# Three edits to a fused attention and expert kernel: every high half of the exponentials on ScalarE, one instruction for both biases of a query unit, and router logits by 8 products of 16 columns

## The chip, the cores and the metric

The kernel runs on one core of a Trainium2 chip. The metric is the device time of one execution in microseconds, as the median of several runs; the profile is one further execution with its own time. PE is the matrix engine (PEld its loading of weights), DVE the vector engine, ACT the scalar engine, POOL the general engine, SP the engine whose queue issues the DMAs here.

## The reference, cut to what matters

Three stages follow each other: linear attention over 4 batches of 8 heads with 576 tokens, a gated MLP, and a mixture of 8 experts with one expert per token.

```python
proj = x @ w_phi                                   # 64 -> 128, for q and for k
proj = proj - max(abs(proj), axis=-1)
phi = concatenate([exp(proj), exp(-proj)])
num = phi(q) @ (phi(k).T @ v);  den = phi(q) . sum(phi(k)) + 1e-6
x = num / den
xn = x / rms(x) * rms_g
x = (silu(xn @ w_gate) * (xn @ w_val)) @ w_out
logits = x @ w_gate2 + modality_bias[modality_id]  # 512 -> 8
out = gate * (relu(x @ w1[e]) @ w2[e])             # e = argmax(logits)
```

## The kernel before, in words

Values that need more than 16 bits are carried as a pair of float16 tiles, a high half (the value cast to float16) and a low half (the value minus its high half), and a product of two pairs is three matmuls: high by high, high by low, low by high. The function `split` (L146 to L152) makes such a pair: the cast on DVE (`hi="v"`, L149) or on ACT (`hi="a"`, L151), then the subtraction on DVE (L152).

**Attention.** Per batch there are 9 key units (`k_unit`) and 9 query units (`q_unit`), each with 4 blocks of 128 features in one bank of the matrix engine's output memory. A key unit takes the largest absolute value on DVE, subtracts it, and ACT takes the two exponentials of half a unit at a time (L301, L302). A query unit takes the maximum (`absmax`, L215), DVE makes two bias columns from it, `b1` = -3 times and `b2` = -1 times the maximum (L351, L352), and ACT takes 4 times 2 exponentials with these biases (L358, L359). Each half unit is then split. For batches 0 and 1 all casts of these splits are on ACT; for batches 2 and 3, by the table `EXP_SPLIT`, the first half unit's cast is on DVE and the second's on ACT. In batch 1 the keys are not split, in batch 0 and 1 all queries are. A DMA transpose (L365, `eT<-eq`) turns the split query unit around, and `oo` multiplies it with the key sums.

**MLP.** Tokens go in 9 groups of 256. Per group and block of 128 of the 1536 hidden features, `m1_mm` does 24 matmuls of 256 columns into `gv` (L520), and `m1_act` makes the hidden block: tanh on ACT (`th`, L527), two products on DVE (`th` L528, `hu` L530), and a split (`hT`). `gv` has two buffers, and the second product `hu` is the last reader of each. `m1_out_mm` multiplies with `w_out` (L542), `m1_evict` and `m1_store` write the result as a pair and transpose it (`x2T`), and `m1_logits` makes the router's logits of 128 tokens by 12 matmuls of 8 columns (L568) and one DVE instruction (L570) that scales and adds the bias table `lgb`. There are 18 such tiles of 128 tokens.

**Weights.** The MLP's weights are unpacked beside batch 0 and 1 (`wst`, `wu`, `wgv`, `wo`). The experts' weights come in 128 pieces, each loaded (`w2a`), cast on ACT (L635), reduced to its low half on DVE (L636), and stored (`w2b`), from batch 1 to the end of the MLP. All DMAs but the experts' gather and scatter are issued by SP in order.

**Experts.** A routing block on DVE sorts the tokens; then 20 or more slots of 128 tokens go through `mm1` (L978) and `mm2` (L994).

**Order.** `_weave` mixes the lists of steps of attention, MLP and weights by fixed shares, and the framework then schedules the whole program by a simulated timeline: the order of each engine's instructions is that schedule's, not the code's. Each engine takes its instructions in that order.

Of the kernel before, what the change touches and what calls it, by code (L numbers as in the profile page):

```python
# [8 lines left out]
F32 = mybir.dt.float32  # L9
# [3 lines left out]
ALU = mybir.AluOpType  # L13
# [9 lines left out]
NE = 8  # L23
# [9 lines left out]


CONV_LO = "v"
EXP_SPLIT = ('av', 'av', 'vv av', 'vv av')
PREP_LO = ('v', 'v', 'v', 'v')
NKV = 8
NXG = 2
# [23 lines left out]
def body(ctx, tc, k0, kt0, q0, qt0, kk, kkt, qq, qqt, vv, vvt, w_phi, w_gv, w_out, rms_g, mid, w_g2, mbias,  # L63
         w1, w2, consts, out):
    nc = tc.nc
    V, A, G, SP, PE = nc.vector, nc.scalar, nc.gpsimd, nc.sync, nc.tensor
# [4 lines left out]
    ps_ko = ctx.enter_context(tc.tile_pool(name="ps_ko", bufs=2, space=PSUM))  # L71
# [7 lines left out]
    def C(name, shape, dt=F32):  # L79
        return cp.tile(shape, dt, name=name)  # L80
# [5 lines left out]
    g_bc = C("g_bc", [128, DM])  # L86
    epsb = C("epsb", [128, 1])
    mhalf = C("mhalf", [128, 1])
    wg32 = C("wg32", [128, 4, NE])
    wg16 = C("wg16", [128, 4, 2, NE], F16)  # L90
    mid_i = C("mid_i", [128, NT, 2], I32)
# [2 lines left out]
    lgb = C("lgb", [128, NT, NE])  # L94
    lg = C("lg", [128, NT, NE])
# [5 lines left out]
    SP.dma_start(out=wp32, in_=w_phi)  # L101
    V.memset(epsb, math.log(0.25e-6))
    V.memset(mhalf, -0.5)

    def small_loads():
        SP.dma_start(out=cst, in_=consts)
        SP.dma_start(out=g_bc, in_=rms_g.rearrange("(o d) -> o d", o=1).to_broadcast([128, DM]))
# [103 lines left out]
    def small(tag, n, bufs=4):  # L211
        return apx.tile([128, n], F32, tag=tag, bufs=bufs, name=tag)

    def absmax(p, m):
        V.tensor_reduce(out=m, in_=p, axis=AX.X, op=ALU.max, apply_absolute_value=True)  # L215

    def attention(b, banks, eng, pp_lo):

        f32 = b == 0
        k32 = b == 1  # L220
        sc = 1.0 if f32 else 0.0625
        t, m, kvs, x = {}, {}, {}, {}
# [3 lines left out]
        def bank():  # L226
            pool, tag = banks[cnt[0] % len(banks)]
            cnt[0] += 1
            return pool.tile([128, 4, 128], F32, tag=tag, name="pj")

        def esplit(hi, lo, src):
            h, l = eng[lo_cnt[0] % len(eng)]
            lo_cnt[0] += 1
            split(hi, lo, src, hi=h, lo=l)
# [89 lines left out]
        def q_unit(p, rp):  # L324

            pp = bank()
            a = t["q", p]
            if p == 4:
                for i in range(4):
                    if f32:  # L330
                        PE.matmul(pp[:, i, :], lhsT=a[:, 128 * i:128 * i + 128], rhs=wp32[0:64, 0, :], start=True, stop=True)
                    else:
                        PE.matmul(pp[:, i, :], lhsT=a[:, i, :], rhs=wpA, start=True, stop=False)
                        PE.matmul(pp[:, i, :], lhsT=a[:, i, :], rhs=wpB, start=False, stop=True)
                mm, ppv, sh = m["t"], pp, lambda y: y
            else:
                for r in range(2):
                    if f32:
                        c = 128 * (2 * rp + r)
                        PE.matmul(pp[:, 2 * r:2 * r + 2, :], lhsT=a[:, c:c + 128], rhs=wp32, start=True, stop=True)  # L340
                    else:
                        for i in range(2):
                            l = a[:, 4 * i + 2 * rp + r, :]
                            PE.matmul(pp[:, 2 * r + i, :], lhsT=l, rhs=wpA, start=True, stop=False)
                            PE.matmul(pp[:, 2 * r + i, :], lhsT=l, rhs=wpB, start=False, stop=True)
                mm = m["m"][:, 2 * rp:2 * rp + 2, 2 * p:2 * p + 2]
                ppv = pp.rearrange("p (r h) f -> p r h f", h=2)
                sh = lambda y: y.rearrange("p (r h) -> p r h", h=2)
            absmax(ppv, mm)
            b1, b2 = small("b1", 4), small("b2", 4)  # L350
            V.tensor_scalar(out=sh(b1), in0=mm, scalar1=-3.0 * sc, scalar2=None, op0=ALU.mult)  # L351
            V.tensor_scalar(out=sh(b2), in0=mm, scalar1=-sc, scalar2=None, op0=ALU.mult)  # L352
            eq = ap.tile([128, 2, 4, 2, FEAT], F16, tag="E4", bufs=4, name="eq")
            for half in range(2):
                e = ap.tile([128, 2, 2, FEAT], F32, tag="e32", bufs=2, name="e32")
                for r in range(2):
                    j = 2 * half + r
                    A.activation(out=e[:, r, 0, :], in_=pp[:, j, :], func=AF.Exp, scale=sc, bias=b1[:, j:j + 1])  # L358
                    A.activation(out=e[:, r, 1, :], in_=pp[:, j, :], func=AF.Exp, scale=-sc, bias=b2[:, j:j + 1])  # L359
                sl = slice(2 * half, 2 * half + 2)  # L360
                esplit(eq[:, 0, sl], eq[:, 1, sl], e)
            tag, bufs = ("E4", 4) if cnt[1] % 3 else ("eX", 1)
            cnt[1] += 1
            o = ap.tile([128, 16, 128], F16, tag=tag, bufs=bufs, name="eT")
            SP.dma_start_transpose(out=o, in_=eq.rearrange("p a r s f -> p (a r s f)"))  # L365
            t["eT", p, rp] = o
            if p == 4:
                m["t2"] = apx.tile([64, 4], F32, tag="mt2", bufs=2, name="mt2")
                SP.dma_start(out=m["t2"], in_=m["t"][64:128])
# [88 lines left out]
        for n, h in enumerate(order + [None]):  # L458
            pre = []
            if h is not None and h < 8:  # L460
                p = h // 2
# [15 lines left out]
        def q_steps(rp):  # L477
            st = []
            for p in range(5):
                fs = []  # L480
                if p < 4:
                    fs.append(L(q_unit, p, rp))
                    if rp == 0:
                        if p + 1 < 4:
                            fs.append(L(prep, "q", p + 1))
                        if p + 2 < 4:
                            fs.append(L(load, "q", p + 2))
                    elif p == 0:
                        fs.append(L(load, "q", 4))
                    elif p == 1:  # L490
                        fs.append(L(prep, "q", 4))
                if p < 4:
                    st.append(seq(*fs))
                elif rp == 1:
                    st += [L(q_unit, 4, 0)]
                if p >= 2:
                    st.append(L(oo, p - 2, rp))
            if rp == 1:
                st.append(tail_m)
            st.append(L(oo, 3, rp))  # L500
            st += [seq(L(norm, 2 * rp)), seq(L(norm, 2 * rp + 1), L(ntr, 2 * rp)), L(ntr, 2 * rp + 1)]
            return st
# [58 lines left out]
    def m1_logits(g, i):  # L561
        t = state.pop(("x2T", g, i))
        tt = 2 * g + i
        p = ps_ko.tile([128, NE], F32, tag="ko", name="lgp")
        n = 0
        for kc in range(4):
            for xl, wl in ((0, 0), (0, 1), (1, 0)):
                mm = PE.matmul(p, lhsT=t[:, 4 * xl + kc, :], rhs=wg16[:, kc, wl, :], start=(n == 0), stop=(n == 11))  # L568
                n += 1
        V.scalar_tensor_tensor(out=lg[:, tt, :], in0=p, scalar=1.0 / 1024.0, in1=lgb[:, tt, :],  # L570
                               op0=ALU.mult, op1=ALU.add)
        return mm.ins

    def out_steps(g):
# [12 lines left out]
    def group_steps(g, prev):  # L587

        st = []
        for c in range(12):  # L590
            st.append(lambda c=c: m1_mm(g, c, 0))

            def s(c=c):
                m1_mm(g, c, 1)
                m1_act(g, c)
                if prev is not None:
                    if c == 2:
                        m1_store(prev, 1)
                    if c == 4:
                        m1_logits(prev, 0)  # L600
                    if c == 6:
                        m1_logits(prev, 1)
            st.append(s)
            if c == 1 and prev is not None:
                st += out_steps(prev)
        return st
# [444 lines left out]
    bk = list(wide)  # L1051
    att = [attention(b, bk if b == 0 else narrow, EXP_SPLIT[b].split(), PREP_LO[b]) for b in range(4)]
    done = [0]
# [21 lines left out]
    for b in range(4):  # L1075
# [8 lines left out]
        n = KSPLIT * len(ks) // 100  # L1084
# [9 lines left out]
        n = len(wst) // 2  # L1094
# [14 lines left out]
    n = len(w2s) * M7 // (M7 + 12)  # L1109
# [6 lines left out]
    for s in out_steps(8):  # L1116
        s()
    m1_store(8, 1)
    last = [m1_logits(8, 0), m1_logits(8, 1)]
    moe_ctx.close()  # L1120
    rpools.append(ctx.enter_context(tc.tile_pool(name="rp2", bufs=1, reuse_waits="tile")))
# [90 lines left out]
```

## Time and profile before

| | us |
|---|---|
| median of 3 runs | 919.63 |
| lowest, highest | 914.98, 919.82 |
| profiled execution | 923.65 |
| span of the profile in it | 921.9 |
| busy PE, DVE, ACT in the span | 814.6, 592.9, 431.7 |
| mean granted TensorE clock | 0.935 |

The profiled execution took 1.75 us more than its span, and 4.0 us more than the median. By stage: until about 95 us the attention of batch 0 with little else on PE, until 256 us the MLP of the first groups beside batch 1 and the MLP's own weights, from 256 us to 546 us the MLP beside the keys and queries of batches 2 and 3 and the experts' weights, until 702 us the rest of the MLP, routing and weights, and from then on the experts.

### The profile page before, as it was taken

Reading aid. Unit: us, or ns where it says so; the run is one execution under the profiler, and the core shown is the slowest. Engines: PE = TensorE matmul, PEld = TensorE weight load, DVE = VectorE, ACT = ScalarE, POOL = GpSimd, SP = SyncE. Lnnn points to the kernel's source line nnn. Section 1 sums busy time; section 2 is a strip of 40 time slices with the busy share of each in tenths; the row PEclk is TensorE's granted clock in tenths of the full one; section 3 lists DMA queues with packets and bytes.
Section 4 is the critical chain, followed back from the end, with each engine's and each line's share of the span. In section 5 each row is a group of like instructions: output and inputs, shape, how many; then the busy total and the mean of one; then the engine's idle time right before and its main releaser. Section 6 shows DMA issues by size and latency. Waiting matters only on the chain. (4 is left out here: it accounts for less than half of the span.)

```text
span 921.9 us, 18413 instructions
## 1 busy us (share of the span) xinstructions
PE 814.6 (88%) x6840; PEld 559.0 (61%) x6840; DVE 592.9 (64%) x1448; ACT 431.7 (47%) x1125; POOL 86.8 (9%) x104
## 2 busy tenths in 40 slices
PE   5745789988899998989998979998899998999995
PEld 5534588767577776666786667675674443444442
DVE  6989898996778877869987866456835411122121
ACT  4787555585656665757767744234321111111110
POOL 0001030000130000210000102000010221211010
PEclk8656699999989999999999989999999999999998
DMA  8589978599989799899879986897896499698732
GB/s 268 146 193 217 206 154 207 164 196 234 212 209 260 238 242 241 199 232 242 215 221 232 226 223 190 311 356 247 235 379 136 114 233 217 130 303 240 173 71 52
DMA packets 266589, 197.38 MB, mean 214 GB/s; under 512 B 212863, under 2 KB 214271, under 8 KB 262912
## 3 DMA queue, kind: packets, MB, share of 16 engines
q1 hardware_dynamic: 263296, 186.21, 79.3%
q0 software_dynamic: 3200, 9.97, 3.4%
q8 instruction: 55, 0.90, 0.4%
q14 instruction: 38, 0.31, 0.1%
HBM read 164.92 MB, written 43.52 MB: 226 GB/s over the span
## 5 line engine op out<-in xcount | busy, mean ns | idle before, releaser
L520 PEld LDWEIGHTS <-wgv 128*128 128x128 f16 x2592 | 257.4, 101 | 71.8 <-issue 23.5
L520 PE MATMUL gv<-xT,wgv 128*128 128x256 f16 x2304 | 281.2, 281 | 19.2 <-DVE hu L530 11.8
L542 PE MATMUL po<-wo,hT 128*128 128x512 f16 x648 | 152.1, 380 | 0.3
L635 ACT ACTIVATE w2b<-w2a 128x512 f16<-128x512 f32 x128 | 80.9, 632 | 114.3 <-DMA w2a<-in_w_dram 107.5
L636 DVE SCALAR_TENSOR_TENSOR w2b<-w2a,w2b 128x512 f16<-128x512 f32 x128 | 88.6, 692 | 70.2 <-ACT w2b L635 69.9
L994 PE MATMUL m2y<-L,hsT 128*128 128x512 f16 x480 | 108.4, 383 | 3.9 <-DMA hsT<-hs 3.9
L981 ACT ACTIVATE hs<-m2h 128x512 f16<-128x512 f32 x40 | 23.9, 597 | 180.8 <-PE m2h L978 180.8
L978 PE MATMUL m2h<-L,xT 128*128 128x512 f16 x480 | 107.0, 379 | 0.8 <-DMA L<-ws 0.5
L542 PEld LDWEIGHTS <-hT 128*128 128x128 f16 x648 | 61.2, 98 | 62.7 <-DVE hT L152 1.2
L994 PEld LDWEIGHTS <-hsT 128*128 128x128 f16 x480 | 47.2, 99 | 62.1 <-DMA hsT<-hs 5.1
L978 PEld LDWEIGHTS <-xT 128*128 128x128 f16 x480 | 46.6, 98 | 57.4 <-issue 1.4
L982 DVE SCALAR_TENSOR_TENSOR hs<-m2h,hs 128x512 f16<-128x512 f32 x40 | 27.6, 691 | 79.7 <-ACT hs L981 75.9
L423 POOL TENSOR_TENSOR x<-x,g_bc 128x512 f32<-128x512 f32 x16 | 22.0, 1373 | 483.4 <-ACT xg L422 482.7
L387 PE MATMUL oo<-kv,eT 128*128 128x65 f16 x768 | 33.0, 204 | 35.4 <-DMA eT<-eq 30.1
L151 ACT CAST hT<-hu 128x256 f16<-128x256 f32 x108 | 43.7, 406 | 32.4 <-DVE hu L530 31.1
L528 DVE SCALAR_TENSOR_TENSOR th<-th,gv 128x256 f32<-128x256 f32 x108 | 44.7, 414 | 20.7 <-ACT th L527 20.3
L358 ACT ACTIVATE e<-pj,b 128x128 f32<-128x128 f32 x144 | 55.3, 384 | 4.8 <-DVE eq L152 2.2
L359 ACT ACTIVATE e<-pj,b 128x128 f32<-128x128 f32 x144 | 56.2, 390 | 0.0
L387 PEld LDWEIGHTS <-eT 128*128 128x128 f16 x768 | 30.0, 104 | 42.6 <-DMA eT<-eq 36.5
L527 ACT ACTIVATE th<-gv 128x256 f32<-128x256 f32 x108 | 41.5, 384 | 28.5 <-PE gv L520 28.3
L318 PE MATMUL kv<-vs,ek 128*128 128x65 f16 (+1 forms) x720 | 43.2, 206 | 13.0 <-DVE ek L152 9.9
L152 DVE TENSOR_TENSOR eq<-e,eq 128x512 f16<-128x512 f32 x72 | 52.0, 727 | 3.6 <-ACT eq L151 3.3
(226 smaller groups left out, 1066.2 us busy)
## 6 DMA issues: line engine op xcount, KB each, us to landing
L<-ws SPq DMA_DIRECT2D x88, 1024.0 KB
w2a<-in_w_dram SPq DMA_DIRECT2D x128, 256.0 KB
ws<-w2b SPq DMA_DIRECT2D x128, 256.0 KB
wst<-in_w_gv_dram SPq DMA_DIRECT2D x24, 512.0 KB
wst<-in_w_out_dram SPq DMA_DIRECT2D x12, 512.0 KB
xs<-x SPq DMA_DIRECT2D x18, 256.0 KB
v<-in_vv_dram SPq DMA_DIRECT2D x16, 260.0 KB
k<-in_kk_dram SPq DMA_DIRECT2D x12, 256.0 KB
```

Of the source, the lines that this page charges most:

```text
L151: A.copy(dst_hi, src)
L152: (V if lo == "v" else G).tensor_tensor(out=dst_lo, in0=src, in1=dst_hi, op=ALU.subtract)
L358: A.activation(out=e[:, r, 0, :], in_=pp[:, j, :], func=AF.Exp, scale=sc, bias=b1[:, j:j + 1])
L359: A.activation(out=e[:, r, 1, :], in_=pp[:, j, :], func=AF.Exp, scale=-sc, bias=b2[:, j:j + 1])
L387: PE.matmul(acc[:, j, :], lhsT=et[:, hl * 8 + j * 2 + s, :], rhs=kvs[2 * p + j % 2][:, vl, s, :], start=(n == 0), stop=(n == 5))
L520: PE.matmul(p[:, which, :], lhsT=w[:, kc, wl, f], rhs=x[:, 4 * xl + kc, :], start=(n == 0), stop=(n == 11))
L528: V.scalar_tensor_tensor(out=t, in0=t, scalar=1.0, in1=p[:, 0, :], op0=ALU.add, op1=ALU.mult)
L542: PE.matmul(p, lhsT=hT[g, c][:, hl, tk], rhs=wo[:, c, wl, :], start=(c == 0 and hl == 0 and wl == 0), stop=(c == 11 and hl == 1))
L635: A.activation(out=o[:, :, 0, :], in_=t, func=AF.Copy, scale=WS)
L636: V.scalar_tensor_tensor(out=o[:, :, 1, :], in0=t, scalar=WS, in1=o[:, :, 0, :], op0=ALU.mult, op1=ALU.subtract)
L978: PE.matmul(p, lhsT=x[:, 4 * xl + kc, :], rhs=w[:, kc, half, wl, :], start=(n == 0), stop=(n == 11))
L994: PE.matmul(p, lhsT=t[:, 4 * hl + i, :], rhs=w[:, fc, wl, :], start=(fc == 0 and hl == 0 and wl == 0), stop=(fc == 7 and hl == 1))
```

## The change

Three edits. The table `EXP_SPLIT` now puts the cast of every half unit on ACT, in batches 2 and 3 too (18 casts of each). In a query unit one DVE instruction, a product of the maximum with a constant tile `mneg` (-3 and -1, with the batch's scale), makes both bias columns in one tile `b12`, where two did before; the constants are four small memsets at the start. And `m1_logits` multiplies the high half and the low half of the tokens with the weights' high and low half side by side, 8 matmuls of 16 columns in place of 12 of 8, whose two column groups two DVE instructions add up; the product of the two low halves, which was left out before, is now part of the sum.

```diff
-EXP_SPLIT = ('av', 'av', 'vv av', 'vv av')
+EXP_SPLIT = ('av', 'av', 'av', 'av')
...
+    mneg = [C(f"mneg{i}", [128, 2, 1]) for i in range(2)]
...
+    for i, s in enumerate((1.0, 0.0625)):
+        V.memset(mneg[i][:, 0], -3.0 * s)
+        V.memset(mneg[i][:, 1], -s)
...
-            b1, b2 = small("b1", 4), small("b2", 4)
-            V.tensor_scalar(out=sh(b1), in0=mm, scalar1=-3.0 * sc, scalar2=None, op0=ALU.mult)
-            V.tensor_scalar(out=sh(b2), in0=mm, scalar1=-sc, scalar2=None, op0=ALU.mult)
+            b12 = small("b12", 8).rearrange("p (a n) -> p a n", a=2)
+            b1, b2 = b12[:, 0], b12[:, 1]
+            cn = mneg[0 if f32 else 1]
...
+                V.tensor_tensor(out=b12.rearrange("p a (r h) -> p a r h", h=2),
+                                in0=mm.unsqueeze(1).to_broadcast([128, 2, 2, 2]),
+                                in1=cn.unsqueeze(3).to_broadcast([128, 2, 2, 2]), op=ALU.mult)
...
-        p = ps_ko.tile([128, NE], F32, tag="ko", name="lgp")
+        p = ps_ko.tile([128, 2, NE], F32, tag="ko", name="lgp")
         n = 0
         for kc in range(4):
-            for xl, wl in ((0, 0), (0, 1), (1, 0)):
-                mm = PE.matmul(p, lhsT=t[:, 4 * xl + kc, :], rhs=wg16[:, kc, wl, :], start=(n == 0), stop=(n == 11))
+            for xl in range(2):
+                mm = PE.matmul(p.rearrange("p a e -> p (a e)"), lhsT=t[:, 4 * xl + kc, :],
+                               rhs=wg16[:, kc].rearrange("p a e -> p (a e)"), start=(n == 0), stop=(n == 7))
                 n += 1
-        V.scalar_tensor_tensor(out=lg[:, tt, :], in0=p, scalar=1.0 / 1024.0, in1=lgb[:, tt, :],
-                               op0=ALU.mult, op1=ALU.add)
+        for i, b in ((1, lgb), (0, lg)):
+            V.scalar_tensor_tensor(out=lg[:, tt, :], in0=p[:, i, :], scalar=1.0 / 1024.0, in1=b[:, tt, :],
+                                   op0=ALU.mult, op1=ALU.add)
```

The framework schedules the new program anew, so instructions that the diff does not name move as well. Line numbers of the new kernel are up to 13 higher. The first query unit of batch 2 on DVE, before (`mq` is the maximum, `b` the bias columns, `e` the exponentials, `eq` the split unit, the others belong to the MLP and the weights):

```order
L215 TENSOR_REDUCE mq<-pj 128x2x2
L636 SCALAR_TENSOR_TENSOR w2b<-w2a,w2b 128x512
L351 TENSOR_SCALAR b_4784<-mq 128x4
L352 TENSOR_SCALAR b_4785<-mq 128x4
L528 SCALAR_TENSOR_TENSOR th<-th,gv 128x256
L530 SCALAR_TENSOR_TENSOR hu<-th,gv 128x256
L215 TENSOR_REDUCE mq<-pj 128x2x2
L149 CAST eq<-e_4789 128x512
L351 TENSOR_SCALAR b_4861<-mq 128x4
L352 TENSOR_SCALAR b_4862<-mq 128x4
L152 TENSOR_TENSOR eq<-e_4789,eq 128x512
```

The same unit on DVE in the changed kernel:

```order
L219 TENSOR_REDUCE mq<-pj 128x2x2
L361 TENSOR_TENSOR b_4742<-mq,mneg_82 128x8
L649 SCALAR_TENSOR_TENSOR w2b<-w2a,w2b 128x512
L219 TENSOR_REDUCE mq<-pj 128x2x2
L539 SCALAR_TENSOR_TENSOR th<-th,gv 128x256
L361 TENSOR_TENSOR b_4817<-mq,mneg_82 128x8
L541 SCALAR_TENSOR_TENSOR hu<-th,gv 128x256
L649 SCALAR_TENSOR_TENSOR w2b<-w2a,w2b 128x512
L583 SCALAR_TENSOR_TENSOR lg<-lgp,lgb 128x8
L156 TENSOR_TENSOR eq<-e_4745,eq 128x512
```

The cast between the maximum and the low half is gone, one bias instruction stands for two, and the logits' first sum stands ahead of the low half now. The same unit on ACT, before, from its last exponentials on:

```order
L358 ACTIVATE e_4796<-pj,b_4784 128x128
L359 ACTIVATE e_4796<-pj,b_4785 128x128
L635 ACTIVATE w2b<-w2a 128x512
L151 CAST hT<-hu 128x256
L151 CAST vs<-v_6178 128x8x65
L373 ACTIVATE ep<-mq,epsb 128x4
L151 CAST eq<-e_4796 128x512
L527 ACTIVATE th<-gv 128x256
```

And on ACT in the changed kernel:

```order
L369 ACTIVATE e_4752<-pj,b_4742 128x128
L370 ACTIVATE e_4752<-pj,b_4742 128x128
L538 ACTIVATE th<-gv 128x256
L648 ACTIVATE w2b<-w2a 128x512
L155 CAST eq<-e_4745 128x512
L155 CAST vs<-v_6109 128x8x65
L155 CAST eq<-e_4752 128x512
L384 ACTIVATE ep<-mq,epsb 128x4
```

The cast of the first half unit (`e_4745`), which DVE did before, now stands on ACT behind the second half's exponentials, a tanh and a conversion of expert weights.

## Rows read from the trace of the kernel before

**Rows 1.** The page's first part: busy us, share of the span, instructions per engine.
```profile
PE 814.6 (88%) x6840; PEld 559.0 (61%) x6840; DVE 592.9 (64%) x1448; ACT 431.7 (47%) x1125; POOL 86.8 (9%) x104
```
**Rows 2.** Windows: stretch, length, busy us PE PEld DVE ACT POOL, clock, DMA share, GB/s.
```profile
20.00:60.00 40.00, 27.54 (x266) 20.18 (x266) 39.50 (x86) 31.77 (x86) 0.00 (x0) 0.59 0.62 173
60.00:120.00 60.00, 35.06 (x397) 28.73 (x398) 51.75 (x118) 39.83 (x112) 7.11 (x8) 0.67 0.95 203
120.00:256.00 136.00, 124.08 (x1147) 97.19 (x1146) 114.66 (x270) 83.54 (x224) 9.80 (x14) 0.97 0.85 199
256.00:546.00 290.00, 265.88 (x2852) 205.62 (x2849) 233.86 (x546) 189.25 (x518) 23.24 (x30) 0.98 0.93 229
546.00:702.00 156.00, 145.02 (x1161) 103.92 (x1162) 87.38 (x274) 55.84 (x129) 10.78 (x13) 0.97 0.86 275
702.00:922.00 220.00, 205.45 (x957) 92.62 (x955) 53.26 (x135) 22.92 (x39) 35.66 (x36) 0.98 0.68 166
```
**Rows 3.** Waits of PE from 256 to 546 us: total us, times, longest.
```profile
PE oo L387 <- DMA eT<-eq: 10.0, 7, 3.2
PE gv L520 <- DVE hu L530: 6.9, 7, 2.0
...
PE oo L387 <- DVE th L528: 1.0, 1, 1.0
PE oot L411 <- DMA eT<-eq: 0.7, 1, 0.7
PE pj L284 <- ACT e L302: 0.6, 1, 0.6
```
**Rows 4.** Longest waits of DVE and of ACT, same stretch.
```profile
DVE w2b L636 <- ACT w2b L635: 38.0, 40, 3.3
...
ACT w2b L635 <- DMA w2a<-in_w_dram: 64.4, 49, 3.9
```
**Rows 5.** Waits of PE from 20 to 120 us.
```profile
PE oo L387 <- DMA eT<-eq: 20.2, 7, 6.9
```
**Rows 6.** PE in order of time: start, us, instruction, count [idle before]; three places.
```profile
302.72 2.04 PE L318 MATMUL kv<-vs,ek 128*128 128x65 f16 x44
...
698.31 0.45 PE L568 MATMUL lgp<-wg,x2T 128*128 128x8 f16 x12
698.61 2.75 PE L978 MATMUL m2h<-L,xT 128*128 128x512 f16 x12
```
**Rows 7.** Instruction groups by line and form, 256 to 546 us: busy, mean ns | idle before.
```profile
L635 ACT ACTIVATE w2b<-w2a 128x512 f16<-128x512 f32 x79 | 50.0, 632 | 66.7 <-DMA w2a<-in_w_dram 64.4 <-DVE th L528 0.8 <-ACT kv L320 0.7
...
L151 ACT CAST eq<-e 128x512 f16<-128x512 f32 x17 | 10.6, 623 | 0.1
L151 ACT CAST ek<-e 128x512 f16<-128x512 f32 x17 | 10.5, 619 | 0.2
L149 DVE CAST ek<-e 128x512 f16<-128x512 f32 x18 | 7.5, 416 | 0.2 <-ACT e L302 0.2
L149 DVE CAST eq<-e 128x512 f16<-128x512 f32 x17 | 7.2, 424 | 2.0 <-ACT e L359 1.8
```
**Rows 8.** DVE in order of time, a query unit of batch 2.
```profile
345.67 0.42 DVE L149 CAST eq<-e 128x512 f16<-128x512 f32 x1
346.00 0.16 DVE L351 TENSOR_SCALAR b<-mq 128x4 f32<-128x4 f32 x1
346.07 0.16 DVE L352 TENSOR_SCALAR b<-mq 128x4 f32<-128x4 f32 x1
```
**Rows 9.** ACT in order of time, a cast of a split between others.
```profile
304.80 0.61 ACT L151 CAST ek<-e 128x512 f16<-128x512 f32 x1
305.32 0.38 ACT L527 ACTIVATE th<-gv 128x256 f32<-128x256 f32 x1
```
**Rows 10.** The logits' sum on DVE, group by line over the span.
```profile
L570 DVE SCALAR_TENSOR_TENSOR lg<-lgp,lgb 128x8 f32<-128x8 f32 x18 | 2.9, 159 | 4.2 <-PE lgp L568 4.2
```

More of the change, by code (lines that the diff above doesn't have):

```diff
@@ L349, in q_unit @@
             absmax(ppv, mm)
-            b1, b2 = small("b1", 4), small("b2", 4)
-            V.tensor_scalar(out=sh(b1), in0=mm, scalar1=-3.0 * sc, scalar2=None, op0=ALU.mult)
-            V.tensor_scalar(out=sh(b2), in0=mm, scalar1=-sc, scalar2=None, op0=ALU.mult)
+            b12 = small("b12", 8).rearrange("p (a n) -> p a n", a=2)
+            b1, b2 = b12[:, 0], b12[:, 1]
+            cn = mneg[0 if f32 else 1]
+            if p == 4:
+                V.tensor_tensor(out=b12, in0=mm.unsqueeze(1).to_broadcast([128, 2, 4]),
+                                in1=cn.to_broadcast([128, 2, 4]), op=ALU.mult)
+            else:
+                V.tensor_tensor(out=b12.rearrange("p a (r h) -> p a r h", h=2),
+                                in0=mm.unsqueeze(1).to_broadcast([128, 2, 2, 2]),
+                                in1=cn.unsqueeze(3).to_broadcast([128, 2, 2, 2]), op=ALU.mult)
             eq = ap.tile([128, 2, 4, 2, FEAT], F16, tag="E4", bufs=4, name="eq")
```

## The prediction

> **What bounds the kernel now.** First the busy times [rows 1]: PE is busy for 814.6 of 921.9 us, no other engine for two thirds of it. Then the windows by stage [rows 2], because the three edits sit in different stages. From 702 us on PE is busy for 205.5 of 220 us and DVE for 53: nothing that happens on DVE or ACT matters there. From 20 to 60 us DVE is full (39.5 of 40) and PE is not, at a granted clock of 0.59. From 60 to 120 us PE waits most for the transposed query units (20.2 us in 7 waits [rows 5]), with the DMA engines at 0.95. From 120 to 546 us PE is the fullest engine again. The cast edit acts in one stretch, 256 to 546 us: 35 of the 36 casts that move stand there [rows 7]. PE idles for 290.0 - 265.9 = 24.1 us of it, DVE is busy for 233.9 and ACT for 189.3. So this is the ceiling: what the cast edit can win is a part of 24.1 us, and PE's waits say which part [rows 3]. 10.7 us end on transposed query units (10.0 and 0.7), 7.9 us on DVE products of the MLP (6.9 and 1.0), and only 0.6 us directly on ACT. Last the other engines' waits [rows 4]: ACT stands for 64.4 us with a weight conversion at its head whose load has not come, and DVE for 38.0 us behind ACT for the same pieces. Both have spare time, but it is spare time at the head of an ordered queue: everything queued behind waits too.
>
> **The logits.** 12 matmuls of 8 columns take 0.30 us from the first to the next matmul on PE (698.31 to 698.61 [rows 6]), 25 ns each. The 18 tiles drop 4 matmuls each. What a matmul of 16 columns takes, the trace does not show; the neighbours are 8 columns at 25 ns and 65 columns at 46 ns (44 in 2.04 us [rows 6]). At 25 ns a tile takes 0.20 us and the 18 save 1.8 us; at 46 ns it takes 0.37 us and they cost 1.2 us. I take 25 ns, since 16 is much nearer to 8. The Trainium skill, "TensorE: Matmul & The Clock Gate", section on the 56 ns gap, states that start-to-start does not fall below about 25 ns and gives that for 32 columns too; by it the sum would be the same 1.8 us. PE is the fullest engine where the tiles lie, so I count the saving in full: **-1.8 us**. The second sum on DVE costs 18 times between 0.07 us (the step between two small instructions in a row, 346.00 to 346.07 [rows 8]) and 0.16 us [rows 10], at most 2.9 us of DVE time over the whole span. It holds the logits' output buffer that much longer, of which there are two. The last two tiles lie at 698 and 701 us, where DVE is mostly idle and PE has expert matmuls to do. I count it at nothing; without that cover it would be 0.16 us for the last tile.
>
> **The biases.** Two small instructions in a row take 0.16 us each but start 0.07 us apart [rows 8], so dropping one of them frees 0.07 us of DVE, not 0.16: 36 times 0.07 = 2.5 us, half of it in batches 2 and 3. A product of 128x8 elements is taken as one of the same kind; between 0 and 0.07 us more would eat the gain. For the units of batch 0, in the stretch where DVE is full, it is less than 0.7 us, and the transposes after it are paced by the DMA queue. I count the first two batches at nothing. The four memsets stand at the start, where DVE waits for the first loads anyway.
>
> **The casts.** On DVE a cast lasts 0.42 us [rows 7] and holds the engine for 0.33 us (345.67 to 346.00 [rows 8]); on ACT it lasts 0.62 us and holds the engine for 0.52 us (304.80 to 305.32 [rows 9]). So DVE loses 36 x 0.33 = 11.9 us, with the biases 1.3 us more, less 0.6 us for the eight second sums in this stretch: 233.9 becomes 221.3 us of 290. ACT gains 36 x 0.52 = 18.7 us: 189.3 becomes 208.0, still below DVE. PE's 24.1 us of idle time can't vanish by that, since no cast is on PE; what shrinks is the time for which work that PE needs stands queued on DVE. I estimate that from the ratio of busy to idle time: 233.9/56.1 = 4.2 before, 221.3/68.7 = 3.2 after, 23% less. Of PE's waits, 7.9 us end on a DVE product and 10.7 us on a transpose, whose issue follows the last DVE instruction of its unit: 23% of 18.6 us is **-4.3 us**. This is the softest number here; its bounds are 0 (the waits stay as they are, because another order makes others) and two thirds of 18.6, -12.4 us.
>
> Against it stands the longer cast: +0.20 us between the exponentials and the low half. PE waited for a transpose 8 times in this stretch [rows 3], and half of the splits before were on ACT already, so four of these waits grow by 0.2 us: **+0.8 us**. The low half on DVE now waits for ACT; behind it on DVE stand the MLP's products and the low halves of weights, which is the price of a late ACT (below). No DMA is added and none is moved by the text of the diff; SP's queue gets the same instructions in a new order, and POOL's are unchanged in number.
>
> **The sum:** -1.8 - 4.3 + 0.8 = -5.3 us. The profiled execution would go from 923.65 to 918.3 us. It lies 4.0 us above the median of the runs, so for the median I take 919.63 - 5.3 = **914.3 us**. The schedule is made anew for the whole program, which adds a spread that no row prices; I let the bounds above stand for it.
>
> **Rivals.** *Only the logits count.* PE's waits stay in sum, because what DVE gains is spent in front of weight conversions (38.0 us of DVE's waiting is for those [rows 4]) and none of it reaches PE. For it: DVE's idle time is nearly all such waiting. Against it: 7.9 us of PE's waits do end on DVE. 919.6 - 1.8 = 917.8 us.
>
> *ACT becomes late (slower).* In the new order on ACT the first cast of the unit shown stands behind the second half's exponentials, a tanh and a weight conversion, where DVE took it at once before. Counted over the orders, 31 weight conversions stood between a half unit's last exponential and its cast on ACT before, and 45 do now: 14 more. Such a conversion costs the queue (50.0 + 64.4)/79 = 1.45 us on average, load included [rows 4, 7]. That is 20.3 us of later casts. PE was waiting at 8 of the 18 transposes of batches 2 and 3, so I let half of it through: +10.2 us. With the logits and half of DVE's gain, -1.8 - 2.2 + 10.2 = +6.2: 925.8 us. It turns the sum into a loss once a fifth of those 20.3 us reaches PE, since that is the 4.0 us that the logits and half of DVE's gain give. For it: ACT's head is blocked for 64.4 us already. Against it: DVE was blocked on the same pieces through ACT, so the old cast on DVE stood behind them as well, only elsewhere. The Trainium skill, "ScalarE: Activation LUTs", rules for kernel authors, says to use VectorE rather than ScalarE for plain arithmetic, since VectorE is faster per element. The trace agrees on the size, 0.42 against 0.62 us [rows 7], and for this change it points to this rival.
>
> *The waits fall by more.* If two thirds of the 18.6 us go, -1.8 - 12.4 + 0.8: 906.2 us.
>
> *The logits don't get cheaper*, 46 ns a matmul: 3.0 us more than any case above; I keep it inside the ranges.
>
> **How the numbers follow.** The forecast 0.42, with an own range of 910 to 918; only the logits 0.24; late ACT 0.24; more 0.10. About 0.5% (4.6 us, 915.0 and 924.2) is what a measurement of this kernel can tell from no change. Faster: 0.30 of the forecast's share, the 0.10, and 0.03 of the second case, 0.43. Slower: 0.21 of late ACT's share and 0.01, 0.22. The rest, 0.35, is the same. The range reaches from the strongest gain to late ACT, 906 to 926.
>
> **What would show it.** Right: 8 matmuls per logits tile in 0.20 us; DVE 12 to 13 us and PE's idle time about 3 to 5 us lower in the stretch of batches 2 and 3; ACT 18 to 19 us busier there; the waits of `gv` for `hu` and of `oo` for `eT` together well below 18.6 us. Wrong: those waits at or above 18.6 us with casts on ACT behind weight conversions (late ACT); the same sum with DVE's waiting for weight conversions up by the 12 us (only the logits); a logits tile of 0.30 us or more; or a difference that lies before 256 or after 546 us, where I count nearly nothing.

## The result and the profile after

The changed kernel is slower: 931.93 us (median of 4 runs, 930.95 to 934.91) against 919.73 us for the kernel before in the same comparison, a ratio of 1.0139 with a 95% interval of 1.0091 to 1.0187. The profiled execution took 930.95 us with a span of 929.1, against 923.65 and 921.9 before, so the two traces differ by 7.3 us and show a good half of the 12.2 us between the medians. Executions more than 1.5% above the fastest of their kernel are left out of all ratios here.

The first part of the page after (busy us, share of the span, instructions) answers to [rows 1]:

```profile
PE 816.3 (88%) x6768; PEld 559.0 (60%) x6768; DVE 582.1 (63%) x1398; ACT 450.7 (49%) x1161; POOL 89.6 (10%) x104
```

DVE is 10.8 us less busy, ACT 19.0 us more, PE the same. The windows of the kernel after, with the columns of [rows 2]:

```profile
0.00:20.00 20.00, 11.41 (x72) 10.73 (x72) 14.01 (x33) 9.49 (x22) 0.19 (x4) 0.94 0.88 293
20.00:60.00 40.00, 27.66 (x264) 20.52 (x261) 38.98 (x81) 31.93 (x85) 0.00 (x0) 0.59 0.57 161
60.00:120.00 60.00, 35.06 (x388) 29.04 (x389) 50.56 (x115) 40.28 (x109) 7.68 (x9) 0.64 0.95 204
120.00:256.00 136.00, 125.70 (x1120) 97.00 (x1119) 112.17 (x253) 83.45 (x222) 9.83 (x13) 0.96 0.78 192
256.00:546.00 290.00, 258.26 (x2713) 196.93 (x2714) 221.17 (x497) 203.43 (x552) 25.61 (x30) 0.95 0.91 226
546.00:702.00 156.00, 145.87 (x1209) 108.78 (x1208) 88.77 (x282) 56.81 (x130) 10.66 (x13) 0.98 0.86 277
```

From 256 to 546 us DVE fell from 233.9 to 221.2 us and ACT rose from 189.3 to 203.4, and yet PE's idle time rose from 24.1 to 31.7 us. The granted clock of the stretch is 0.95, where it was 0.98 before. That difference does not explain the loss: it is 0.97 in `casts` below, which loses as much, and 0.95 and 0.96 in `pin_relief` and `pin_before`, which lose nothing. The waits of PE in that stretch, as in [rows 3]:

```profile
PE oo L398 <- DMA eT<-eq: 11.7, 8, 2.5
PE gv L531 <- DVE hu L541: 7.5, 5, 3.5
PE gv L531 <- DMA xT<-xg: 4.6, 2, 3.3
PE oot L422 <- DMA eT<-eq: 3.9, 1, 3.9
PE pj L337 <- ACT e L370: 2.2, 1, 2.2
PE pj L348 <- ACT e L370: 0.9, 1, 0.9
```

What ends on transposed query units grew from 10.7 to 15.6 us, what ends on exponentials from 0.6 to 3.1 us, and what ends on the MLP's DVE products stayed (7.9 and 7.5 us). Transposes and products together stand at 23.1 us, above the 18.6 us of before: the sign that the prediction had set for a late ACT. The longest waits of DVE and ACT, as in [rows 4], both fell, from 38.0 and 64.4 us:

```profile
DVE w2b L649 <- ACT w2b L648: 31.8, 30, 2.9
ACT w2b L648 <- DMA w2a<-in_w_dram: 45.7, 43, 3.4
```

So ACT spends 18.7 us less in front of conversions, as the prediction supposed, and PE idles longer all the same. Where the MLP stands can be read from ACT in order of time: ACT writes `x` from the MLP's last products once for each token tile; the second such row of a group is a mark of the MLP's progress. Three marks of before (start, us, instruction):

```profile
249.20 0.58 ACT L549 ACTIVATE x<-po 128x512 f16<-128x512 f32 x1
...
468.69 0.60 ACT L549 ACTIVATE x<-po 128x512 f16<-128x512 f32 x1 [0.48 <-PE po L542]
...
695.97 0.60 ACT L549 ACTIVATE x<-po 128x512 f16<-128x512 f32 x1 [2.47 <-PE po L542]
```

The same three of after:

```profile
254.44 0.58 ACT L560 ACTIVATE x<-po 128x512 f16<-128x512 f32 x1
...
477.43 0.62 ACT L560 ACTIVATE x<-po 128x512 f16<-128x512 f32 x1
...
704.51 0.60 ACT L560 ACTIVATE x<-po 128x512 f16<-128x512 f32 x1 [0.70 <-PE po L553]
```

The MLP is 5.2 us late at the first mark, before any cast that moved matters, 8.7 us at the second and 8.5 us at the third. The first mark does not show that PE has lost time by then. The window of before that [rows 2] leaves out:

```profile
0.00:20.00 20.00, 11.53 (x66) 10.78 (x66) 12.44 (x26) 8.57 (x20) 0.19 (x4) 0.95 0.82 258
```

With it PE is busy for 198.2 of the first 256 us before and for 199.8 after, and has 616.4 and 616.5 us of busy time still ahead. From 546 to 702 us it idles for 11.0 and 10.1 us, and behind that for 14.4 and 14.8. So what moved ahead of 256 us is the MLP's place among the other work, and the idle time that PE gained lies in the stretch from 256 to 546 us. Last the logits, PE in order of time:

```profile
710.98 0.35 PE L579 MATMUL lgp<-wg,x2T 128*128 128x16 f16 x8
711.18 3.18 PE L991 MATMUL m2h<-L,xT 128*128 128x512 f16 x14
```

Eight products take 0.20 us from their start to the next product's, as forecast from [rows 6].

### The profile page after: what moved, and what is told of

Read it like the earlier page. It is cut to its first block, busy times and chain, and to the rows that moved or that the text cites. A ratio compares the mean times of both kernels' runs of the same rounds, so it can differ in the third digit from the quotient of the medians.

```text
span 929.1 us, 18238 instructions
## 1 busy us (share of the span) xinstructions
PE 816.3 (88%) x6768; PEld 559.0 (60%) x6768; DVE 582.1 (63%) x1398; ACT 450.7 (49%) x1161; POOL 89.6 (10%) x104
## 5 line engine op out<-in xcount | busy, mean ns | idle before, releaser
L156 DVE TENSOR_TENSOR eq<-e,eq 128x512 f16<-128x512 f32 x72 | 49.8, 697 | 10.0 <-ACT eq L155 9.7
```

Of the source, the lines that this page charges most:

```text
L156: (V if lo == "v" else G).tensor_tensor(out=dst_lo, in0=src, in1=dst_hi, op=ALU.subtract)
```

## The experiments

All ratios are to the kernel before, run on the same chip in the same comparison, with 95% intervals. The median of the kernel before was between 919.7 and 924.1 us in the comparisons, so times of different ones are not set against each other; where ratios of different ones are, the text says so.

**Each edit alone, scheduled anew.** `casts` has only the new `EXP_SPLIT`, `bias` only the `mneg` tiles and the one product, `logits` only the 16-column products and the second sum. `swap` does exactly before's work; two source lines change places:

```
-            V.tensor_scalar(out=sh(b1), in0=mm, scalar1=-3.0 * sc, scalar2=None, op0=ALU.mult)
             V.tensor_scalar(out=sh(b2), in0=mm, scalar1=-sc, scalar2=None, op0=ALU.mult)
+            V.tensor_scalar(out=sh(b1), in0=mm, scalar1=-3.0 * sc, scalar2=None, op0=ALU.mult)
```

> Only the table: the 36 casts of batches 2 and 3 move to ACT, the schedule is made anew. The first 250 us keep before's order. Theory late ACT: the whole loss of the changed kernel is here, 928 to 932 us, and lies after 256 us. Theory order (the loss is not in the work but in the new order that the schedule takes): any value from 914 to 928, with the first 250 us as in before.

> Only the biases: one instruction for two in 36 query units, four memsets at the start. It takes 2.5 us of DVE away and adds nothing anywhere. Late ACT: no change, 918 to 920 us. Order: the schedule differs from the first query unit on, so the about 5 us that the changed kernel has lost by 163 us show here; 922 to 928 us although the work is less.

> Only the logits: 8 matmuls of 16 columns for 12 of 8 in 18 tiles, a second sum on DVE. Late ACT: 917.9 us, the 1.8 us of the prediction. Order: 1.8 us less from the work and up to 8 us either way from the new order after 225 us. In both a logits tile takes 0.20 us on PE; 0.30 or more if 16 columns are dearer than 8.

> The work of the kernel before, word for word, with the two bias instructions of a query unit written in the other order: the schedule comes out differently, nothing else does. Late ACT: 919.7 us, within 0.3%. Order: it differs from before by 3 us or more, either way, by the order alone.

Measured: `casts` 1.0136 [1.0076, 1.0195], `bias` 1.0056 [1.0016, 1.0095], `logits` 0.9999 [0.9959, 1.0039], `swap` 1.0026 [0.9992, 1.0060]. The casts alone give a loss as large as that of the whole change. But `bias`, which takes 36 small instructions away and adds four memsets, is slower too, and at the first mark it stands where the kernel after does, and so does `swap` (`bias` first):

```profile
254.29 0.58 ACT L560 ACTIVATE x<-po 128x512 f16<-128x512 f32 x1
...
255.23 0.58 ACT L549 ACTIVATE x<-po 128x512 f16<-128x512 f32 x1
```

A smaller program that runs longer points to the new order. `swap` shows no difference in time that its interval can tell from none, so not every new order has a cost that shows, and a late first mark is no measure of it. Apart from the two lines themselves, its trace keeps before's order on ACT and DVE until about 192 us.

**Work and order apart.** The next kernels fix the order. At the end of the body the instructions of each engine, as written, are chained in the order of a list by edges that carry no semaphore:

```
+    for one, two in zip(order, order[1:]):
+        tc.add_manual_dep(mine[two], mine[one].name,
+                          mybir.DependencyInfo(mybir.DependencyClass.NoSync, mybir.DependencyReason.DATA),
+                          reason="order")
```

In the `pin_` kernels the list is the order of the kernel before; an added or moved instruction stands behind the one that precedes it in the source on its engine, so a cast that moved to ACT follows its half unit's exponentials directly, with no weight conversion between. In the traces of all nine `pin_` kernels, here and below, ACT, DVE, PE and SP take what the edits left alone in before's order. `pin_before` is the control, `pin_casts` has the casts alone, `pin_after` all three edits. `rev_before` is the reverse: before's work in the order of the kernel after.

> A control: the kernel before with its own order fixed by edges between neighbours on each engine. All theories: 919.7 us, within 0.3%.

> All three edits, but in the order of the kernel before: a moved cast stands on ACT right behind its half unit's last exponential, one bias instruction where the first of two stood, 8 logits matmuls where 12 stood, the second sum behind the first; nothing else moves. Order: the edits' work shows alone, the 5.3 us of the prediction's sum, 912 to 917 us. Late ACT: ACT has its 18.7 us more here too, 925 us or more.

> Only the moved casts, in the order of the kernel before. Order: -3.5 us by the prediction (relief of DVE less the longer cast), 913 to 919 us. Late ACT: 925 us or more, all the loss of the changed kernel but no loss before 256 us.

> The work of the kernel before in the order of the changed one: a cast of batches 2 and 3 stands on DVE right ahead of its low half, two bias instructions where one stood, 12 logits matmuls where 8 stood. Order: as slow as the changed kernel or slower by the 5.3 us that the edits' work saves, 932 to 940 us. Late ACT: the loss goes with the casts, 917 to 923 us.

Measured: `pin_before` 0.9977 [0.9943, 1.0010], so the edges cost nothing that can be measured. `pin_casts` 1.0045 [1.0016, 1.0074], where the same casts scheduled anew were 1.0136 in another comparison. `pin_after` 1.0067 [1.0029, 1.0104], where the kernel after is 1.0139. `rev_before` 1.0226 [1.0183, 1.0270]: before's own work loses over 2% in the other order. Its row for 256 to 546 us, then that of `pin_before`:

```profile
256.00:546.00 290.00, 252.22 (x2710) 192.50 (x2706) 235.25 (x534) 183.63 (x507) 26.13 (x30) 0.97 0.91 222
```

```profile
256.00:546.00 290.00, 267.09 (x2833) 206.62 (x2832) 233.30 (x541) 187.72 (x513) 22.92 (x30) 0.96 0.94 228
```

DVE and ACT have the same load in both and the granted clock is no lower in the first, and PE idles for 37.8 against 22.9 us. So the order alone can cost more than the whole change does. The work in the old order costs too, though less.

**What in the casts costs, with the order fixed or free.** `pin_relief` gives DVE its relief without loading ACT: the 36 casts are left out of DVE, and POOL writes zeros in the place of these high halves, so the low halves of those exponentials carry the whole value:

```
-            V.tensor_copy(dst_hi, src)
+            G.memset(dst_hi, 0.0)
```

`pin_dummy` is the opposite: all casts stay where they were, and behind each of the 36 on DVE ACT casts the same half unit into a tile that nobody reads:

```
             V.tensor_copy(dst_hi, src)
+            A.copy(spare, src)
```

`no_casts` has the biases and the logits, scheduled anew; `pin_no_casts` has the same in before's order.

> In the order of the kernel before, the 36 casts of batches 2 and 3 on DVE are left out, and ACT gets nothing for them: the high half of these half units is set to zero on the idle POOL, so the low half carries the value in one float16. This is DVE's relief by 12 us alone, and a chain that is 0.42 us shorter. Prediction's term: -4.3 us. If DVE's relief is worth nothing (DVE waits for weight conversions instead): within 2 us of the kernel before in its own order. Late ACT says nothing on it.

> In the order of the kernel before, all casts stay where they were, and ACT makes 36 more casts into a tile that nothing reads, each right behind its half unit's last exponential. This is ACT's 18.7 us alone: no longer chain, no relief. If ACT's occupation is what costs: as slow as the moved casts in this order or slower, +4 to +8 us. If it is the longer chain of the unit: within 2 us of the kernel before.

> The changed kernel without its casts on ACT (biases and logits edited, schedule made anew). Late ACT: the loss is gone, 917 to 920 us. Order: the first 250 us are those of the changed kernel, about 5 us late, so 923 to 930 us.

> Biases and logits edited, in the order of the kernel before. By the prediction -1.8 us, all from the logits: 915 to 919 us. If the logits cost more than they save (16 columns dearer, the second sum in DVE's way): 921 us or more, which would also account for what all three edits in this order cost beyond the casts.

Measured: `pin_relief` 0.9979 [0.9950, 1.0008], the same as the control: 10 us of DVE time bring nothing. `pin_dummy` 1.0042 [1.0007, 1.0076], the same as `pin_casts`, with no chain longer and DVE unrelieved; its interval overlaps those of `pin_relief` and of the control by a hair. `pin_no_casts` 0.9981 [0.9954, 1.0008], the control again, and `no_casts` 1.0049 [1.0014, 1.0084], the same work in a new order. The windows, 256 to 546 us, of `pin_relief` and of `pin_dummy`:

```profile
256.00:546.00 290.00, 266.49 (x2843) 206.74 (x2844) 223.57 (x510) 187.78 (x517) 39.65 (x63) 0.95 0.93 231
```

```profile
256.00:546.00 290.00, 261.05 (x2759) 200.70 (x2760) 232.87 (x538) 207.19 (x548) 23.28 (x30) 0.96 0.91 224
```

PE is as busy in `pin_relief` as in `pin_before`, though DVE is 9.7 us less so. In `pin_dummy` ACT has 19.5 us more and PE 6.0 us less. What PE waits for, `pin_before` first (its last row is DVE's longest wait):

```profile
PE oo L387 <- DMA eT<-eq: 10.5, 7, 4.3
PE gv L520 <- DVE hu L530: 8.2, 7, 2.5
PE gv L520 <- DMA xT<-xg: 1.7, 2, 1.0
PE kv L318 <- DVE ek L152: 1.1, 1, 1.1
PE oot L411 <- DMA eT<-eq: 0.7, 1, 0.7
...
DVE w2b L636 <- ACT w2b L635: 39.0, 38, 3.4
```

The same of `pin_relief`:

```profile
PE oo L387 <- DMA eT<-eq: 11.1, 5, 3.8
PE gv L520 <- DVE hu L530: 6.4, 6, 2.5
...
PE oot L411 <- DMA eT<-eq: 2.7, 1, 2.7
...
DVE w2b L636 <- ACT w2b L635: 40.1, 40, 3.2
```

The waits on transposes and on `hu`, which the prediction let shrink by 23%, come to 20.2 us against 19.4, and DVE waits no longer for conversions than before. The zeros on POOL hide no gain that the trace shows: no low half of `eq` or `ek` waits for POOL, and `hu` lasts 414 ns against 415. The waits of PE in `pin_dummy`:

```profile
PE oo L389 <- DMA eT<-eq: 11.8, 7, 3.4
PE gv L522 <- DVE hu L532: 8.4, 9, 2.8
PE gv L522 <- DMA xT<-xg: 3.7, 3, 2.3
PE kv L320 <- DVE ek L154: 1.7, 1, 1.7
PE pj L286 <- ACT e L304: 1.2, 1, 1.2
PE pj L346 <- ACT e L361: 0.8, 2, 0.6
```

No one wait carries the loss: five kinds grow by 0.6 to 2.0 us each. The spare time at ACT's head takes most of the added work. ACT's longest wait, `pin_before` and `pin_dummy`:

```profile
ACT w2b L635 <- DMA w2a<-in_w_dram: 70.3, 55, 4.0
```

```profile
ACT w2b L637 <- DMA w2a<-in_w_dram: 54.4, 46, 3.3
```

ACT has 19.5 us more to do and spends 15.9 us less in that wait, and PE is 6.0 us less busy all the same. That what stands behind on ACT (exponentials, tanh, casts of the transposed operands) starts later each time is the likely reason; no run shows it by itself.

**The other way round.** If ACT's load set the time by its amount, relieving ACT would gain. `pin_actrelief` leaves out ACT's 36 casts in batches 2 and 3 (POOL writes zeros as above); `pin_vv` moves these to DVE, and `vv` does so with a new schedule; `pin_vv_all` adds the biases and the logits in before's order:

```
-EXP_SPLIT = ('av', 'av', 'vv av', 'vv av')
+EXP_SPLIT = ('av', 'av', 'vv', 'vv')
```

> In the order of the kernel before, the 36 casts of batches 2 and 3 that were on ACT already are left out: the high half of these half units is set to zero on the idle POOL, so the low half carries the value in one float16. ACT gets 18.7 us less, DVE the same. If ACT's occupation sets the time by its amount, both ways: -0.4 to -0.6%, 914 to 916 us where the kernel before is at 919.7. If only work added on top of the tuned order costs: within 0.2%.

> The table turned the other way: all casts of batches 2 and 3 on DVE, each right ahead of its low half, in the order of the kernel before. ACT loses 18.7 us, DVE gains 11.9 us. If ACT's occupation costs and DVE's is free, as 12 us less on DVE brought nothing: -0.4 to -0.6%. If DVE's idle time is needed too: +0.3% or more.

> The same table, all casts of batches 2 and 3 on DVE, with the schedule made anew. ACT's occupation alone would give -0.4 to -0.6%; a new order has cost between 0 and 0.6% with nearly equal work, so -0.6 to +0.3%. If casts are dear on either engine once they are moved: +0.5% or more.

> The candidate for a better kernel: all casts of batches 2 and 3 on DVE, with the edits to biases and logits, in the order of the kernel before. By ACT's occupation -0.4 to -0.6%, by the logits up to -0.2% more: 912 to 916 us. If moved casts are dear on either engine: 922 us or more.

Measured: `pin_actrelief` 1.0019 [0.9986, 1.0052], `pin_vv` 1.0021 [0.9985, 1.0057], `vv` 1.0122 [1.0079, 1.0164], `pin_vv_all` 1.0045 [1.0010, 1.0081]. The window of `pin_actrelief`:

```profile
256.00:546.00 290.00, 264.31 (x2852) 205.68 (x2853) 236.68 (x546) 170.87 (x482) 39.83 (x64) 0.97 0.94 231
```

ACT is 16.9 us less busy than in `pin_before`, and PE is no busier. So ACT's amount of work does not set the time in both directions, and the theory falls in that form. More work on ACT in this order costs 0.4% to 0.5% against the kernel before, and less work on either engine brings nothing that shows. Nor are the casts free on DVE: `pin_vv` can't be told from the kernel before, but `pin_vv_all` and `pin_no_casts` differ in these casts alone, and their intervals, from two comparisons, don't overlap (1.0045 against 0.9981). That is the outcome set down beforehand for casts that are dear on either engine once they are moved. And `vv`, which adds nothing to ACT, loses 1.2% with a new schedule, where the same casts in the old order are at 1.0021.

The pairs side by side (same work; order of before fixed, and scheduled anew):

| work | before's order | scheduled anew |
|---|---|---|
| biases and logits | 0.9981 | 1.0049 |
| casts | 1.0045 | 1.0136 |
| casts the other way | 1.0021 | 1.0122 |
| all three edits | 1.0067 | 1.0139 |

In the first three pairs the intervals don't overlap; in the last they just do (1.0104 and 1.0091). A fifth pair, `pin_before` and `swap`, has the same sign and overlaps (0.9977 and 1.0026). The casts and all three edits have their two numbers from different comparisons, and the left column has the edges too, which by the control are worth -0.23% with an interval from -0.57% to +0.10%. What a new schedule settles beside the order, such as the buffer that a tile gets, was not tried apart from it. No kernel of these is faster than the one before by more than its interval.

## Why the prediction was wrong

The forecast was -5.3 us and slower had a chance of 0.22; the result is +12.2 us, outside the range of 906 to 926. Three steps failed: DVE's relief was worth nothing, ACT's load was priced far too low, and the new schedule had no term at all.

**The logits, -1.8 us: the price was right, the saving can't be seen.** A tile takes 0.20 us. `logits` and `pin_no_casts` are within 0.2% of one and of the control; 1.8 us is 0.2%, less than their intervals tell apart.

**The biases, 0: right as work.** In before's order, together with the logits, they cost nothing that can be measured. The one product of 128x8 elements lasts 157 ns, about as long as each of the two small ones did (0.16 us [rows 8]):

```profile
L361 DVE TENSOR_TENSOR b<-mq,mneg 128x8 f32<-128x8 f32 x16 | 2.4, 157 | 0.0
```

That the edit reorders the program from batch 0 on was not priced; `bias` alone is at 1.0056.

**DVE's relief, -4.3 us: this term was wrong.** I took PE's waits that end on DVE, or on a transpose behind it, to shrink with DVE's ratio of busy to idle time. DVE fell to 221.2 us as forecast, and in `pin_relief` to 223.6 with POOL's zeros as the only work added, and the time did not move: 0.9979 against 0.9977 of the control, where -4.3 us would be -0.47%, at the edge of what the two intervals leave open. The waits that were to shrink did not (20.2 against 19.4 us). What ends a wait names the last link only: by the program the `hu` that PE waits for stands behind a tanh on ACT and behind PE's own products. Of the rivals, the one that gives DVE's gain no weight was right on this point, but not by its mechanism: DVE's wait for conversions took up 1.1 of the 9.7 us in `pin_relief` and fell in the kernel after. Nor was DVE's idle time "nearly all" such waiting before; it was 38.0 of 56.1 us.

**ACT's load, +0.8 us: too small by a factor of 5 to 8.** I priced only the longer chain, and let 18.7 us of occupation vanish in ACT's 64.4 us of spare time. `pin_dummy` costs 0.65% more than the control and `pin_casts` 0.68%, about 6 us (4 us against the kernel before itself), with no longer chain in the first. That spare time was taken up nearly as supposed, and still PE lost. The Trainium skill, "ScalarE: Activation LUTs", rules for kernel authors, advises plain arithmetic on VectorE rather than ScalarE. These runs agree that the move to ScalarE costs, though the engine was far from full (189 of 290 us); that the opposite move pays, they don't show (`pin_vv` 1.0021).

**The schedule: a term that was left out.** I wrote that a new schedule adds a spread and let the other bounds stand for it. The pairs above show 0.7% to 1.0% for it, 6 to 9 us, in four cases out of four with the same sign. Up to 0.2% of that may belong to the edges. The new order also moves the first mark, before 256 us, where I counted nothing. In twelve traces that follow before's order up to there (the kernel before, `casts`, `vv` and the nine `pin_` kernels, of which three have the new biases in that part) it lies between 247.3 and 252.8 us; in the six whose order differs earlier it lies between 254.3 and 255.6. Four of these differ from about 48 us on (the kernel after, `bias`, `no_casts`, `rev_before`), `swap` from about 192 us and `logits` from about 235 us. But `swap` and `logits` are not measurably slower, and PE's busy time before 256 us is no lower in the kernel after, so the mark shows a new order and not its price.

**The late-ACT rival, 925.8 us,** gave the sign, and nearly the time of `pin_after` (0.67% above the median, 925.9 us). That is a coincidence in part: it rested on casts behind weight conversions, and in `pin_after` none stands ahead of a moved cast. Whether the 14 more conversions ahead of casts are part of what the new order costs was not tried by themselves. They are not needed for a loss: `vv` has no such cast on ACT in batches 2 and 3 and loses 1.2%, and `rev_before` has as many conversions between these exponentials and their casts on ACT as the kernel before, 19 by a count in the traces, casts and exponentials of batches 2 and 3 paired in order (31 in the kernel after), and loses most.

**The sum as measured,** in parts of the kernel before: the edges -0.23%, all three edits in the old order +0.90%, the new order +0.72%, together 1.39%. The order's part rests on two comparisons whose intervals overlap at their ends, and it includes whatever the edges were worth. It isn't one number either: after's order costs 0.7% with the work it was made for, and 2.5% with before's (`rev_before` against the control).

What stays open is why the order of the kernel before is better than five of the seven that were scheduled anew (`logits` and `swap` can't be told from it), and which of its places count. The order after differs from it from batch 0 on, and PE's lost time is spread over five to six kinds of waits. That less work in the fixed order brings nothing, while more work costs, fits an order made for just this work; no run shows the reason.

## What to carry to other kernels

Where a scheduler orders the program, an edit of one line is two edits, the work and a new order; fix the order to price the work, and give the new order a term of its own, whose sign need not be neutral: here it was a loss wherever it could be told from nothing. An engine that stands idle for a third of a stretch can still pass on part of what is added to it; ACT's idle time here lay mostly at the head of its ordered queue. A wait that ends on an engine is no proof that making that engine less busy shortens it.

## What was not expected of the hardware

A product of 16 columns costs 25 ns from start to start (8 in 0.20 us), the same as one of 8 columns (12 in 0.30 us). Two independent instructions of 128x4 elements on DVE and one of 128x8 take 0.16 us each, so by [rows 8] joining two saves the 0.07 us between their starts. The cast of a half unit on ACT lasted longer in the kernel after than before, 661 and 631 ns on average for queries and keys against 623 and 619 [rows 7]:

```profile
L155 ACT CAST ek<-e 128x512 f16<-128x512 f32 x36 | 22.0, 631 | 0.0
L155 ACT CAST eq<-e 128x512 f16<-128x512 f32 x34 | 21.9, 661 | 0.0
```

That goes with the order and not with the number of casts: `pin_after`, with as many of them on ACT in before's order, shows 624 and 620 ns, and `casts`, scheduled anew, 662 and 638. Why is open.

The executions of one fixed program are less alike than the differences asked about: the kernel before alone ran from 915.4 to 929.0 us in 28 runs on one chip, so a difference of 0.2% to 0.4% takes many runs of both.
